# A fused transformer block, forward and backward: two weight transposes and two gates move, and the b2 gradient is summed by ScalarE

## The chip, the cores and the metric

The kernel runs on one core of one Trainium2 chip. TensorE (PE in the profile, with its weight loads as PEld), VectorE (DVE), ScalarE (ACT), GpSimd (POOL) and SyncE (SP) each run their own instructions in order and wait for each other through semaphores. SP, POOL and ACT also issue the DMAs. The metric is the device time of one execution in microseconds, taken as the median of several.

## The reference

The program computes the output of one pre-layernorm block and the gradients of its inputs and weights for a given output gradient (sequence S = 2048, width D = 512, F = 1792, 32 heads of 16; all bf16):

```python
q, k, v = qkv[0], qkv[1], qkv[2]                 # of layernorm(x) @ wqkv
idx = pos[:, None] - (arange(8) * 2)[None, :]    # each row sees itself and 7 earlier rows, 2 apart
logits = where(idx >= 0, einsum("bhsd,bhswd->bhsw", q, k[idx]) * scale, -1e9)
h  = x + einsum("bhsw,bhswd->bhsd", softmax(logits), v[idx]) @ wo
h2 = h + (gelu(layernorm(h) @ w1 + b1) @ w2 + b2)
out, vjp = jax.vjp(f, x, wqkv, wo, w1, b1, w2, b2)
return out, *vjp(grad_out)
```

The gradient of b2 is the sum of grad_out over all 2048 rows: 512 numbers.

## The kernel before, in words

The sequence is cut into four chunks of 512 rows (c = 0 to 3), each of four tiles of 128 rows. The forward pass, about the first 300 us, interleaves the attention of one chunk with the feed-forward part of the one before. For a chunk, `f_attn` forms products of q and k on DVE (L313), sums them on PE against a selection matrix (L320), and makes the softmax on DVE and ACT; the attention weights go to a DRAM buffer `at_r` (POOL queue, L442). `f_o` reads them back in another layout (`a4`, four SP DMAs, L300), multiplies with rows of v on DVE (`pbo`, L330), sums on PE (L336), copies on ACT (L451) and transposes. `f_h` adds the residual and makes the second layernorm. `f_ffn1` is the first FFN matmul with the activation spread over ACT (L508, L510, L518) and DVE (L515, L516, L520); the tensors u, s and g are stored to DRAM for the backward pass. `f_ffn2` is the second FFN matmul (L535).

Between the chunks of the forward pass, `turn_w` transposes the three blocks of wqkv and then wo on PE (L492), copies them on ACT (L493) and stores them for the last stage. The SBUF room of wqkv (tag `wq`) is later that of `w2T`, so w2T can only be written when the last read of wqkv is over. `w2T` and `w1T`, the transposed FFN weights for the backward pass, are each made by one DMA that transposes on its way (L602, L632). Both are issued on the SP queue.

The backward pass has three parts. From about 293 to 505 us, `b1_gg` and `b1_gx` go back through the FFN chunk by chunk in the order 3, 0, 1, 2: `make_goutT` transposes a chunk of the output gradient `gout` on PE into PSUM and copies it out on ACT (`to_T`, two copies of 1024 columns per chunk, L276); then come matmuls with w2T (L697), DVE work, transposes (L706) and matmuls with w1T (L719). `gw2_gen` fills in the gradient of w2 (L667), for which SP loads `gtm` by transposing DMAs (L664). At its start it also makes the gradient of b2: 16 matmuls with a column of ones as the weights (L659), a copy (L660) and a store (L661). Then the attention's backward pass follows: products on DVE (L330) with sums on PE, copied by ACT into `gt` (`b_sum`, L861 and L863), with the gradients of w1, wo and wqkv as fill on PE (L788, L918, L929). At the end `b_gx` (L892) makes the input gradient; for chunks 2 and 3 two of its three operands come through DRAM: a store to `gq_d` (POOL, L875) and a transposing DMA into `gTo` (SP, L876).

The order on each engine is fixed when the program is built: a scheduler moves instructions by priority, so an edit in one place can change the order around it. SP's DMAs also stand in one fixed order, and a DMA that waits holds back those behind it. `gate(ins, key)` adds a wait of `ins` for an earlier instruction recorded in `mark`; it is used to begin a transfer later than its data would allow.

Of the kernel before, what the change touches and what calls it, by code (L numbers as in the profile page):

```python
# [10 lines left out]
P = 128  # L11
BF16 = mybir.dt.bfloat16
F32 = mybir.dt.float32
ACT = mybir.ActivationFunctionType
ALU = mybir.AluOpType
AX = mybir.AxisListType
# [9 lines left out]
CH = 512  # L26
# [9 lines left out]
def kernel(  # L36
# [20 lines left out]
    nc = tc.nc  # L57
# [4 lines left out]
    S, D = xf.shape  # L62
    F = B_w1.shape[1]
    NT = S // P
    NC = S // CH
    TC = CH // P
    DC = D // P
# [7 lines left out]
    scale = DH ** -0.5  # L75

    def pool(name, bufs, side="left", space=None):
        kw = {} if space is None else {"space": space}
        return tc.alloc_tile_pool(name=name, bufs=bufs, side=side, reuse_waits="tile", **kw)
# [10 lines left out]
    const = ctx.enter_context(tc.tile_pool(name="const", bufs=1))  # L90
# [4 lines left out]
    def acc(name, tag="A"):  # L95
        return psum.tile([P, CH], F32, name=name, tag=tag, bufs=1 if tag in "TU" else 2)

    def ptile(name, tag="T"):
        return psum.tile([P, 8 * P], BF16, name=name, tag=tag, bufs=1 if tag in "TU" else 2)
# [4 lines left out]
    sync, pq = nc.sync, nc.gpsimd  # L104
    mark = {}
# [5 lines left out]
    def gate(ins, key):  # L111
        behind(ins, mark[key])


    ident = const.tile([P, P], BF16, name="ident")
# [7 lines left out]
    nc.vector.memset(one_t[:], 1.0)  # L123
    ones_row = const.tile([1, P], BF16, name="ones_row")
    nc.vector.memset(ones_row[:], 1.0)
    ones_col = const.tile([P, 1], BF16, name="ones_col")
    nc.vector.memset(ones_col[:], 1.0)
    rstd1 = const.tile([P, NT], F32, name="rstd1")
    rstd2 = const.tile([P, NT], F32, name="rstd2")
    b1c = const.tile([P, FT], F32, name="b1c")  # L130
# [26 lines left out]
    def pv(d_t):  # L157
        return d_t[:, :].rearrange("p (t d) -> p t d", t=TC)
# [26 lines left out]
    fw = pool("fw", 1, side="right")  # L185
# [79 lines left out]
            nc.vector.tensor_scalar(out=dst[:, j, :], in0=src[:, j, :], scalar1=mv[:, j, 0:1],  # L265
                                    scalar2=r[:, j:j + 1], op0=ALU.subtract, op1=ALU.mult)

    def to_T(src, dst, nm, tag, tag2=None):
        for d2 in range(DC // 2):
            pt = ptile(f"pt{nm}{d2}", tag2 if tag2 and d2 else tag)  # L270
            for i in range(2):
                for j in range(TC):
                    dc = 2 * d2 + i
                    nc.tensor.transpose(pt[:, (i * TC + j) * P:(i * TC + j + 1) * P],  # L274
                                        src[:, j, dc * P:(dc + 1) * P], ident[:])
            nc.scalar.copy(out=dst[:, 2 * d2:2 * d2 + 2, :], in_=pt[:].rearrange("p (i t) -> p i t", i=2))  # L276


    def four(eng, pool_, d_t, t0, nj, name, tag, bufs, step, key=None):
# [177 lines left out]
    def f_h(c):  # L457
        x, oT = load_x(c, "xr"), oTs.pop(c)
        h = fb.tile([P, TC, D], BF16, name=f"h{c}", tag="h", bufs=2)
        for j in range(TC):  # L460
            ps = acc(f"psh{c}_{j}")
            for g in range(G):
                nc.tensor.matmul(ps[:], lhsT=oT[:, g, j * P:(j + 1) * P], rhs=wo[:, g, :], start=(g == 0), stop=(g == G - 1))
            nc.vector.tensor_tensor(out=h[:, j, :], in0=ps[:], in1=x[:, j, :], op=ALU.add)
        ln2 = fr.tile([P, TC, D], BF16, name=f"ln2_{c}", tag="t1", bufs=1)
        layernorm(h, ln2, rstd2, c, "b")
        pq.dma_start(out=pv(ln2_d[c]), in_=ln2[:])
        ln2T = fl.tile([P, DC, CH], BF16, name=f"ln2T{c}", tag="ln2T", bufs=2)
        to_T(ln2, ln2T, f"b{c}", "U")
        hs[c], l2T[c] = h, ln2T  # L470
# [71 lines left out]
    def take(gen, n=1):  # L542
        for _ in range(n):
            next(gen, None)
# [46 lines left out]
    f_h(1)  # L591
    f_attn(2)
    turn_w = turn_w_gen()
    take(turn_w, 2)
    zero_pads(((q_r, S), (go_r, S), (at_r, S), (gl_r, S)), ("e", 1, 0))
    mix(f_ffn1(1), f_ffn2(0))
    f_o(2)
    f_h(2)
    take(turn_w, 2)
    f_attn(3)  # L600
    w2T = fw.tile([P, DC, F], BF16, name="w2T", tag="wq", bufs=1)
    gate(sync.dma_start_transpose(out=w2T[:], in_=B_w2[:, :]), ("e", 3, 1))  # L602
    mix(f_ffn1(2), f_ffn2(1))
    f_o(3)
    f_h(3)
# [1 line left out]
    br1 = pool("br1", 1, side="right")  # L607
    b1_order = (3, 0, 1, 2)
    gout, goutT = {}, {}
# [3 lines left out]
    place(br1, [P, TC, 2 * P], BF16, "th", 3)  # L613
    place(br1, [P, NT, P], BF16, "gtm", 2)
    place(br1, [P, D], BF16, "ow2", 3)
    gb2 = br1.tile([1, D], BF16, name="gb2")
    for c in b1_order:
        gout[c] = br1.tile([P, TC, D], BF16, name=f"gout{c}")
    br2 = pool("br2", 1, side="right")

    def load_gout(c):
# [4 lines left out]
    def make_goutT(i):  # L626
        if i < NC:
            c = b1_order[i]
            goutT[c] = get(br1, [P, DC, CH], BF16, f"goutT{c}", "goutT", 2)
            to_T(gout[c], goutT[c], f"e{c}", "T")  # L630

    w1T_load = sync.dma_start_transpose(out=w1T[:], in_=B_w1[:, :])  # L632
    gate(w1T_load, ("r", 3))
    mix(f_ffn1(3), f_ffn2(2))
    fl.release()

# [17 lines left out]
        nc.vector.tensor_tensor(out=out_ap, in0=u[:], in1=resid, op=ALU.add)  # L654

    def gw2_gen():
        ps = acc("psb2", "A")
        for t in range(NT):
            nc.tensor.matmul(ps[0:1, :], lhsT=ones_col[:], rhs=gout[t // TC][:, t % TC, :], start=(t == 0), stop=(t == NT - 1))  # L659
        nc.scalar.copy(out=gb2[:], in_=ps[0:1, :])  # L660
        nc.scalar.dma_start(out=out_7.rearrange("(a d) -> a d", a=1), in_=gb2[:])  # L661
        for ft in range(FT):
            gtm = get(br1, [P, NT, P], BF16, f"gtm{ft}", "gtm", 2)
            sync.dma_start_transpose(out=gtm[:], in_=g_d[ft * P:(ft + 1) * P, :])  # L664
            ps = acc(f"psw2{ft}", "U")
            for t in range(NT):
                nc.tensor.matmul(ps[:], lhsT=gtm[:, t, :], rhs=gout[t // TC][:, t % TC, :],  # L667
                                 start=(t == 0), stop=(t == NT - 1))
            ow = get(br1, [P, D], BF16, f"ow2{ft}", "ow2", 3)
            nc.scalar.copy(out=ow[:], in_=ps[:])  # L670
            pq.dma_start(out=out_6[ft * P:(ft + 1) * P, :], in_=ow[:])
            yield
# [100 lines left out]
    def load_tmx(f0, nf):  # L773
        tag = ("tm0", "tm2", "tm6", "tm2")[(f0 + 2) // 4]
        tmx = tmxs[f0] = (bg if f0 == 6 else bt).tile([P, NT, nf * P], BF16, name=f"h1tm{f0}", tag=tag, bufs=1)
        pq.dma_start(out=tmx[:], in_=tm(h1tm_d[:, f0 * P:(f0 + nf) * P]))
# [29 lines left out]
    for i in range(1, NC):  # L806
        load_ln2a(i)
        for n, _ in enumerate(b1_gg(i)):
            take(gw2, 1 if n in (2, 5) else 0)
            if n == 3 and i == 1:  # L810
                gate(sync.dma_start(out=woT[:], in_=wo_d[:, :].rearrange("p (j d) -> p j d", j=DC)), ("y", 1, 3))
        if i == NC - 1:
            br2.release()
            bt = pool("bt", 1)
            load_tmx(0, 2)
            load_tmx(2, 4)
            mix(b_go(0), none)
            b_ga(0)
        for n, _ in enumerate(b1_gx(i)):
            take(gw2, 1 if n == 1 else 0)  # L820
        if i > 1:
            mix(b_go(3 if i == 2 else 1), none)
# [24 lines left out]
    def b_sum(c, sel):  # L847
        sg = 0 if sel == 0 else 1
        d_a = at_r if sel == 2 else gl_r
        d_r, t_r = ((k_r, PAD - 2), (q_r, 0), (go_r, 0))[sel]  # L850
        nja = CJ + 2 * sg
        a4 = att4(bs_, d_a, CJ * c, nja, f"ba{sel}_{c}", "ba", 2, sg)
        gt = gvt[c] if sel == 2 else bp.tile([P, TC, D], BF16, name=f"gt{sel}_{c}")
        gts[sel, c] = gt
        for qd in range(Q4):
            r4 = row4(bs_, d_r, qd, t_r + CJ * c, CJ + 2, f"r4_{sel}{c}{qd}", "w4", W4B, sg)
            ps = acc(f"pss{sel}{c}_{qd}", "A")
            wsum(bs_, ps, a4, r4, sg, f"{sel}{c}_{qd}", 200)
            o_ap, i_ap = gt[:, :, qd * P:(qd + 1) * P], ps[:].rearrange("p (j m) -> p j m", j=TC)
            if sel == 2:  # L860
                mark["s", c, 2] = mark["s", c, 2, qd] = nc.scalar.copy(out=o_ap, in_=i_ap)  # L861
            else:
                mark["s", c, sel] = nc.scalar.activation(out=o_ap, in_=i_ap, func=ACT.Copy, scale=scale)  # L863
            yield

    gTs, rooms = {}, []

    def b_gT(c):

        if not rooms:  # L870
            rooms.append(bg.tile([P, NC, DC, CH], BF16, name="gTo", tag="tm6", bufs=1))
        for i, sel in enumerate((2, 0)):
            gTs[sel, c] = rooms[0][:, 2 * (c % 2) + i]
            d_t = gq_d[sel][c]
            gate(pq.dma_start(out=d_t[:, :].rearrange("(j p) d -> p j d", p=P), in_=gts[sel, c][:]), ("s", 2, 1))  # L875
            gate(sync.dma_start_transpose(out=gTs[sel, c], in_=d_t[:, :]), ("s", 3, 1))  # L876

    def b_gx(c):
        gT = {}
# [57 lines left out]
    for c in range(NC):  # L937
# [4 lines left out]
        if c == 2:  # L942
            load_otm()
            load_ln1a(bl, (0, 1, 2), ("g", 3, 0))
            for sel in range(3):
                gate(pq.dma_start(out=wqkvT[:, sel * DC:(sel + 1) * DC, :],
                                  in_=wqkv_d[sel][:, :].rearrange("p (j d) -> p j d", j=DC)), ("g", 3, 0))
# [12 lines left out]
    wg, wq, wk = gwqkv_gen(2), gwqkv_gen(0), gwqkv_gen(1)  # L960
# [54 lines left out]
```

## Time and profile before

| | us |
|---|---|
| median of 5 runs | 714.5 (714.32 to 716.25) |
| the profiled execution | 714.81 |
| its span | 712.3 |
| PE / DVE / ACT / POOL busy | 629.3 / 556.2 / 395.4 / 210.6 |
| w2T transposing DMA: issue, landing | 211.2, 16.6 after |
| w1T transposing DMA: issue, landing | 261.8, 17.3 after |
| first matmul with w2T / with w1T | 293.7 / 321.8 |
| the b2 gradient's matmuls | 338.2 to 345.9 |
| gTo transposing DMAs: issue | 670.0 to 680.4 |

Times in the profile count from the start of the span. A group's line reads: source line, engine, operation, output<-input, shapes, count, then busy time, mean duration of one in ns, and the idle time of the engine just before with what ended it. A timeline's line reads: start, duration, engine, line, operation, and in brackets the idle time before it and what ended that. "SPq" rows are DMA issues on the SP queue. Line numbers in all profile rows are those of the kernel that was profiled.

### The profile page before, as it was taken

What the parts mean: (1) busy time and instruction counts of PE and PEld (TensorE: products, weight loads), DVE (VectorE), ACT (ScalarE), POOL (GpSimd) and SP (SyncE); (2) the same over time, 40 slices, a digit from 0 to 9 for tenths busy, and PEclk for the clock granted to TensorE, in tenths of its full rate; (3) what the DMA queues carried; (4) which work ended last, traced back from release to release, by engine and by line L of the source; (5) the groups of instructions that cost most, each with busy time, mean ns of one, the idle gap of its engine ahead of it and who ended that gap; (6) DMA issues with size and microseconds to landing.
All of it is one profiled execution on the core that took longest, in us unless ns stands there. A gap on an engine that the chain in (4) does not pass through costs nothing. (4 is left out here: it accounts for less than half of the span.)

```text
span 712.3 us, 10332 instructions
## 1 busy us (share of the span) xinstructions
PE 629.3 (88%) x3682; PEld 265.1 (37%) x3682; DVE 556.2 (78%) x919; ACT 395.4 (56%) x548; POOL 210.6 (30%) x318
## 2 busy tenths in 40 slices
PE   1898667779789489999999999998999999999985
PEld 0433222234334134444444444443533333334432
DVE  6467958778972858975988888476899999999754
ACT  5554334878957639945867687552131135357543
POOL 4324333434433443443452433313200410001000
PEclk9999897979989789999999999999999999999999
DMA  8497698664879659567674985859899999986642
GB/s 237 137 266 236 179 367 290 225 260 155 247 295 242 205 162 218 180 197 277 185 222 107 181 209 142 263 108 239 301 354 365 322 344 290 351 284 209 165 102 67
DMA packets 103221, 163.57 MB, mean 230 GB/s; under 512 B 60961, under 2 KB 69250, under 8 KB 103170
## 3 DMA queue, kind: packets, MB, share of 16 engines
q1 hardware_dynamic: 73824, 78.40, 39.7%
q0 software_dynamic: 24720, 80.07, 34.5%
q10 hardware_dynamic: 4626, 4.46, 1.9%
q8 instruction: 28, 0.46, 0.3%
q14 instruction: 23, 0.19, 0.1%
HBM read 90.97 MB, written 56.71 MB: 207 GB/s over the span
## 5 line engine op out<-in xcount | busy, mean ns | idle before, releaser
L330 DVE TENSOR_TENSOR pb<-ba,r 128x2048 bf16<-128x2048 bf16 x96 | 111.5, 1220 | 0.8 <-PE pss L336 0.7
L506 PE MATMUL psf<-ln2T,w 128*128 128x512 bf16 x224 | 59.0, 400 | 12.3 <-ACT u L508 12.2
L535 PE MATMUL ps<-w,g 128*128 128x512 bf16 x224 | 55.7, 379 | 0.0
L788 PE MATMUL psw<-h1tm,ln2a 128*128 128x512 bf16 (+1 forms) x256 | 54.3, 354 | 0.0
L667 PE MATMUL psw<-gout,gtm 128*128 128x512 bf16 x208 | 51.3, 379 | 2.4 <-DMA gtm<-g_d 1.6
L719 PE MATMUL psx<-w1T,gh 128*128 128x512 bf16 x216 | 50.4, 379 | 0.0
L330 DVE TENSOR_TENSOR pbo<-a,v 128x2048 bf16<-128x2048 bf16 x32 | 38.2, 1217 | 15.1 <-DMA a<-at_r 10.2
L372 ACT CAST qkv<-psq 128x512 bf16<-128x512 f32 x48 | 27.6, 586 | 33.3 <-PE psq L370 26.5
L697 PE MATMUL psg<-goutT,w2T 128*128 128x512 bf16 x168 | 42.3, 379 | 0.0
L508 ACT ACTIVATE u<-psf,b1c 128x512 bf16<-128x512 f32 x56 | 36.1, 682 | 8.6 <-PE psf L506 5.3
L506 PEld LDWEIGHTS <-w 128*128 128x128 bf16 x224 | 21.0, 101 | 42.1 <-issue 24.7
L710 POOL DMA_DIRECT2D h1tm_d<-th x27 | 20.9, 772 | 52.5 <-ACT th L708 37.6
L518 ACT ACTIVATE s<-z 128x1024 bf16<-128x1024 bf16 x28 | 29.6, 1060 | 10.5 <-DVE z L516 7.3
L863 ACT ACTIVATE gt<-pss 128x512 bf16<-128x512 f32 x32 | 19.1, 597 | 28.9 <-PE pss L336 28.9
L313 DVE TENSOR_TENSOR pag<-go,bv 128x2048 bf16<-128x2048 bf16 x24 | 28.6, 1219 | 8.2 <-PE ga L320 4.5
L708 ACT COPY th<-pth 128x1024 bf16<-128x1024 bf16 x27 | 27.0, 1000 | 11.1 <-PE pth L706 11.1
L788 PEld LDWEIGHTS <-ln2a 128*128 128x128 bf16 x256 | 22.6, 98 | 27.6 <-issue 10.2
L689 ACT ACTIVATE by<-bu 128x1024 bf16<-128x1024 bf16 x21 | 22.2, 1057 | 19.1 <-DVE gb1p L699 16.4
L929 PE MATMUL psq<-gt,ln1a 128*128 128x512 bf16 x128 | 32.0, 380 | 0.0
L892 PE MATMUL psy<-wqkvT,gT 128*128 128x512 bf16 x128 | 31.8, 379 | 0.3 <-DVE lua L653 0.2
L526 POOL DMA_DIRECT2D g_d<-g x28 | 20.5, 733 | 37.1 <-DVE g L520 35.0
L336 PE MATMUL pss<-pb,sel 128*32 128x512 bf16 x384 | 29.5, 384 | 0.7 <-DVE pb L330 0.5
(221 smaller groups left out, 1365.3 us busy)
## 6 DMA issues: line engine op xcount, KB each, us to landing
v<-v_r SPq DMA_DIRECT2D x16, 576.0 KB, 7.1
r<-go_r SPq DMA_DIRECT2D x16, 576.0 KB, 7.8
r<-k_r SPq DMA_DIRECT2D x16, 576.0 KB, 6.4
r<-q_r SPq DMA_DIRECT2D x16, 576.0 KB, 5.1
g_d<-g POOLq DMA_DIRECT2D x28, 256.0 KB, 4.1
h1tm_d<-th POOLq DMA_DIRECT2D x27, 256.0 KB, 4.6
h1tm<-h1tm_d POOLq DMA_DIRECT2D x3, 2048.0 KB, 12.4
x_d<-u POOLq DMA_DIRECT2D x21, 256.0 KB, 5.3
```

The lines of the kernel that those rows point to most:

```text
L330: last = nc.vector.tensor_tensor(out=pr[:], in0=_ap(a_ap, [a_ap.ap[0], [2 * H, CJ], [0, Q4], [1, H]], off=wh * H + (4 * H * wh if sg else 0)),
L336: mm = nc.tensor.matmul(ps[PR * n:PR * n + PR, :], lhsT=sel4[:], rhs=prs[wh][:, TC * n:TC * n + TC, :, :].rearrange("p j d h -> p (j d h)" ...
L506: nc.tensor.matmul(ps[:], lhsT=w1[0][:, dc, ft * P:(ft + 1) * P], rhs=ln2T[:, dc, :], start=(dc == 0), stop=(dc == DC - 1))
L508: nc.scalar.activation(out=u[:, i, :], in_=ps[:], func=ACT.Identity, bias=b1c[:, ft:ft + 1], scale=1.0)
L518: nc.scalar.activation(out=s[:], in_=z[:], func=ACT.Sigmoid, scale=2.0 * GC)
L535: nc.tensor.matmul(ps[:], lhsT=gs[ft // 2][:, ft % 2, j * P:(j + 1) * P], rhs=w2[0][:, ft, :], start=(ft == 0), stop=False)
L667: nc.tensor.matmul(ps[:], lhsT=gtm[:, t, :], rhs=gout[t // TC][:, t % TC, :], start=(t == 0), stop=(t == NT - 1))
L697: nc.tensor.matmul(ps[:], lhsT=w2T[:, dc, ft * P:(ft + 1) * P], rhs=gT[:, dc, :], start=(dc == 0), stop=(dc == DC - 1))
L719: nc.tensor.matmul(ps[:], lhsT=t1s[ft // 2][:, ft % 2, j * P:(j + 1) * P], rhs=w1T[:, ft, :], start=(ft == 0), stop=(ft == FT - 1))
L788: nc.tensor.matmul(ps[:, 0:nf * P], lhsT=ln2a[:, t // TC, t % TC, dc * P:(dc + 1) * P], rhs=tmx[:, t, 0:nf * P], start=(t == 0), stop=(t = ...
L892: nc.tensor.matmul(ps[:], lhsT=gT[sel][:, g, j * P:(j + 1) * P], rhs=wqkvT[:, sel * G + g, :], start=(n == 0), stop=(n == NJ - 1))
L929: nc.tensor.matmul(ps[:], lhsT=ln1a[t // TC][:, t % TC, dc * P:(dc + 1) * P], rhs=gts[sel, t // TC][:, t % TC, :], start=(t == 0), stop=(t ...
```

## The change

The change has four parts.

- Three blocks instead of two are transposed by `turn_w` before `f_ffn1(1)`, and only the fourth, wo, after `f_h(2)`. The w2T DMA is issued before `f_attn(3)`, gated on the last residual addition of chunk 1, instead of after `f_attn(3)` and gated on its last exponential.
- The gate of the w1T DMA is the last copy of `f_o(3)` instead of the second layernorm's rstd of chunk 3.
- The b2 gradient no longer uses PE's matmuls with ones. `to_T` for the output gradients copies 512 columns at a time (four instructions per chunk instead of two), each with an accumulator output that sums over the 512 rows of the chunk. After the last chunk DVE adds the four partial sums and casts, PE transposes the [128, 4] result, ACT copies it and POOL stores it.
- The gTo DMAs of chunk 2 are gated on the first of the last four gt copies, those of chunk 3 on the third, instead of all on the fourth.

```diff
-    ones_col = const.tile([P, 1], BF16, name="ones_col")
-    nc.vector.memset(ones_col[:], 1.0)
...
-    def to_T(src, dst, nm, tag, tag2=None):
+    def to_T(src, dst, nm, tag, tag2=None, sums=None):
...
-            nc.scalar.copy(out=dst[:, 2 * d2:2 * d2 + 2, :], in_=pt[:].rearrange("p (i t) -> p i t", i=2))
+            if sums is None:
+                nc.scalar.copy(out=dst[:, 2 * d2:2 * d2 + 2, :], in_=pt[:].rearrange("p (i t) -> p i t", i=2))
+            else:
+                for i in range(2):
+                    nc.scalar.activation(out=dst[:, 2 * d2 + i, :], in_=pt[:, i * CH:(i + 1) * CH], func=ACT.Copy,
+                                         accum_out=sums[:, 2 * d2 + i, :])
...
-            nc.vector.tensor_tensor(out=h[:, j, :], in0=ps[:], in1=x[:, j, :], op=ALU.add)
+            mark["h", c] = nc.vector.tensor_tensor(out=h[:, j, :], in0=ps[:], in1=x[:, j, :], op=ALU.add)
...
     turn_w = turn_w_gen()
-    take(turn_w, 2)
+    take(turn_w, 3)
     zero_pads(((q_r, S), (go_r, S), (at_r, S), (gl_r, S)), ("e", 1, 0))
     mix(f_ffn1(1), f_ffn2(0))
     f_o(2)
     f_h(2)
-    take(turn_w, 2)
+    take(turn_w, 1)
+    w2T = fw.tile([P, DC, F], BF16, name="w2T", tag="wq", bufs=1)
+    gate(sync.dma_start_transpose(out=w2T[:], in_=B_w2[:, :]), ("h", 1))
     f_attn(3)
-    w2T = fw.tile([P, DC, F], BF16, name="w2T", tag="wq", bufs=1)
-    gate(sync.dma_start_transpose(out=w2T[:], in_=B_w2[:, :]), ("e", 3, 1))
...
-    gb2 = br1.tile([1, D], BF16, name="gb2")
     for c in b1_order:
         gout[c] = br1.tile([P, TC, D], BF16, name=f"gout{c}")
+    gb2p = br1.tile([P, DC, NC], F32, name="gb2p")
+    gb2s = br1.tile([P, DC], F32, name="gb2s")
+    gb2b = br1.tile([P, DC], BF16, name="gb2b")
+    gb2r = br1.tile([DC, P], BF16, name="gb2r")
...
-            to_T(gout[c], goutT[c], f"e{c}", "T")
+            to_T(gout[c], goutT[c], f"e{c}", "T", sums=gb2p[:, :, c:c + 1])

     w1T_load = sync.dma_start_transpose(out=w1T[:], in_=B_w1[:, :])
-    gate(w1T_load, ("r", 3))
+    gate(w1T_load, ("o", 3, 3))
...
     def gw2_gen():
-        ps = acc("psb2", "A")
-        for t in range(NT):
-            nc.tensor.matmul(ps[0:1, :], lhsT=ones_col[:], rhs=gout[t // TC][:, t % TC, :], start=(t == 0), stop=(t == NT - 1))
-        nc.scalar.copy(out=gb2[:], in_=ps[0:1, :])
-        nc.scalar.dma_start(out=out_7.rearrange("(a d) -> a d", a=1), in_=gb2[:])
...
         if i == NC - 1:
             br2.release()
             bt = pool("bt", 1)
+            nc.vector.tensor_reduce(out=gb2s[:], in_=gb2p[:], axis=AX.X, op=ALU.add)
+            nc.vector.tensor_copy(out=gb2b[:], in_=gb2s[:])
+            pth = ptile("ptg2", "T")
+            nc.tensor.transpose(pth[0:DC, 0:P], gb2b[:, :], ident[:])
+            nc.scalar.copy(out=gb2r[:], in_=pth[0:DC, 0:P])
+            pq.dma_start(out=out_7.rearrange("(dc p) -> dc p", p=P), in_=gb2r[:])
...
-                mark["s", c, sel] = nc.scalar.activation(out=o_ap, in_=i_ap, func=ACT.Copy, scale=scale)
+                mark["s", c, sel] = mark["s", c, sel, qd] = nc.scalar.activation(out=o_ap, in_=i_ap, func=ACT.Copy, scale=scale)
...
-            gate(sync.dma_start_transpose(out=gTs[sel, c], in_=d_t[:, :]), ("s", 3, 1))
+            gate(sync.dma_start_transpose(out=gTs[sel, c], in_=d_t[:, :]), ("s", 3, 1, 2 * (c - 2)))
```

## The prediction

> **What bounds the kernel now.** I read the page first (busy shares and the 40 slices), then the mean clock and DMA share by stretch, then the timelines of each engine around each transfer that the diff touches. The chain that ended last covers only the final 26 us (it begins at 681.26), so each stage was read from its own timeline. From the page:
>
> ```profile
> PE 629.3 (88%) x3682; PEld 265.1 (37%) x3682; DVE 556.2 (78%) x919; ACT 395.4 (56%) x548; POOL 210.6 (30%) x318
> PE   1898667779789489999999999998999999999985
> DVE  6467958778972858975988888476899999999754
> PEclk9999897979989789999999999999999999999999
> DMA  8497698664879659567674985859899999986642
> ```
>
> No engine bounds all of it. Up to about 260 us (slice 15) PE has holes and a lowered clock: the interleave of attention and FFN is held by waits. From 260 to 505 PE is full (9 in nearly every slice); from 512 to 672 DVE is. The largest hole is after 228 us, seen by stretch (columns: stretch, length, then PE, PEld, DVE, ACT, POOL busy, granted clock, DMA share, GB/s):
>
> ```profile
> 165.00:175.00 10.00, 9.98 (x58) 3.99 (x59) 7.79 (x11) 8.54 (x11) 4.56 (x7) 1.00 0.47 143
> 211.00:220.00 9.00, 8.98 (x52) 3.98 (x51) 5.48 (x11) 5.63 (x8) 3.67 (x7) 1.00 1.07 236
> 220.00:228.00 8.00, 8.00 (x38) 3.46 (x37) 2.48 (x5) 6.84 (x9) 3.64 (x5) 1.00 1.14 216
> 228.00:237.00 9.00, 2.88 (x13) 1.00 (x12) 5.45 (x8) 3.48 (x5) 1.61 (x3) 0.87 0.46 168
> ```
>
> DMA is full from 211 to 228, then all engines starve. The timelines of the SP queue, DVE, ACT and PE say why:
>
> ```profile
> 211.19 9.72 SPq L602 DMA_TRANSPOSE w2T<-in_B_w_dram  x1
> 226.96 2.39 SPq L300 DMA_DIRECT2D a<-at_r  x4
> 231.55 1.23 DVE L330 TENSOR_TENSOR pbo<-a,v 128x2048 bf16<-128x2048 bf16 x1 [6.41 <-DMA a<-at_r]
> 235.48 1.06 ACT L518 ACTIVATE s<-z 128x1024 bf16<-128x1024 bf16 x1 [5.49 <-DVE z L516]
> 237.16 3.57 PE L506 MATMUL psf<-ln2T,w 128*128 128x512 bf16 x8 [6.29 <-ACT u L508]
> ```
>
> The w2T transpose lands 16.6 us after issue. Chunk 3's attention weights are written to at_r by POOL at 215.1 to 217.3, beside it, and read back (`a`) behind it. DVE reaches its product with `a` at 225.1 and waits 6.41; DVE runs in order, so the FFN's `z` stands behind it, then ACT, then PE. The same at_r writes in chunk 2, without a transpose, and then in chunk 3, with it:
>
> ```profile
> DMA to landing us min/median/max: 2.0/2.1/2.4
> DMA to landing us min/median/max: 8.6/8.9/10.2
> ```
>
> The last stage has the like: the gTo transposes are issued once the last gt copy is done, and PE waits.
>
> ```profile
> 670.04 4.45 SPq L876 DMA_TRANSPOSE gTo<-gq_d  x2
> 679.49 1.04 PE L892 MATMUL psy<-wqkvT,gTo 128*128 128x512 bf16 x4 [2.64 <-DMA gTo<-gq_d]
> ```
>
> **The change part by part** (positions in the built program, durations from the profiled execution).
>
> 1. *w2T leaves 211 us.* DVE, ACT and PE all stand still there, so the 6.41 is on the path. Without it: at_r issued by 217.3, landing 2.1, `a` issued over 2.4 and landing 2.4, so ready at about 224, before DVE is free at 225.1. Ends: -8.1 (6.4, and PE's eight matmuls at 237.16 taking 1.9 as elsewhere instead of 3.57 at the clock lowered by the hole) and -1.5 (if at_r lands as the stores at 190 to 200 do, 7.0 to 8.5, though no transpose runs there). The chunk 2 row is the same operation, so I take -6.4. What is late next: the xr loads, of which PE's psh has need only after the sums.
>
> 2. *w2T goes in front of chunk 2's `a` load on SP.* It now waits for the last of wqkv's PE transposes, 16 of which (a third block) move ahead of ffn1(1) and stand inside the first two rows of ffn2(0). The second block ran at 157.4 and 159.1; the third follows after a row's rest, so w2T issues at about 163.2. Behind it on SP stand chunk 2's `a` loads, then v, out and xr. With the old distance from w2T's issue to the usable `a` (231.55 - 211.19 = 20.4), `a` is there at 183.6. DVE used it at 179.61; in the new order pa, g and a z go ahead of it, the z needing ACT's square (done at 181.4), so DVE arrives at about 181.5. Stall: 2.1. Ends: 0 (at_r lands in 2.1 after all, DMA share being 0.47 there) and +6.4 (as before at chunk 3). ACT's two copies (1.02 and 1.07 at 186.6 and 197.8, where ACT is 95 to 100% busy) move to 161 to 165, where it waited 2.0 for PE: 0 to -2.1, I take -1.1. Their 16 matmuls cost PE 16 x 0.06, hidden in the same waits. Together +1.0.
>
> The rows first: at_r's landing grew from 2.1 to 8.9 beside the transpose. The Trainium skill ("DMA: Bandwidth & Descriptors", "Issuing engines are not separate DMA queues") says that DMAs of all issuing engines run on the same 16 DMA engines and interleave, which speaks against the change: a transpose moved is a collision moved. By that rule alone chunk 2 would pay what chunk 3 saves, and the sum would be 5.4 us higher; the DMA share of 0.47 against 1.07 speaks for less.
>
> 3. *w1T's gate* moves from rstd (issue at 261.80) to chunk 3's last L451 copy (251.28, done 251.9), ten us earlier. It lands in 17.3. PE is full from 257.8 and first needs it at 321.8; the stretch 250 to 262 has a DMA share of 0.39. The gout and ln stores around 264 are freed of it, but nobody waits for them. 0; ends -1 and +1 (PE's waits of 0.7 at 262, and the stores of chunk 2's last s and g at 253).
>
> 4. *The b2 gradient leaves PE.* Sixteen matmuls against ones:
>
> ```profile
> L659 PE MATMUL psb<-gout,ones_col 128*1 128x512 bf16 x16 | 4.1, 378 | 0.0
> 343.61 2.32 PE L659 MATMUL psb<-gout,ones_col 128*1 128x512 bf16 x10
> ```
>
> Pipelined, (2.32 - 0.38) / 9 = 0.216 each, so 16 x 0.216 = 3.45, in a stage where PE idles 6.9 us of 215. Ends -3.45 and -1.7 (half soaked up by waits for DVE). I take -3.45. The copy and store of gb2 were beside other work.
>
> 5. *ScalarE's sums.* Per chunk two copies of 1.01 become four of 0.597 plus four accumulator reads of 0.196 (ACT's L646 rows; the pair takes 0.69 back to back): 2.76 against 1.9, +0.9. For the first two chunks ACT is 93% busy (290 to 300) and PE waits for these copies already:
>
> ```profile
> 296.91 0.61 PE L274 MATMUL pte<-ident,gout 128*128 128x128 bf16 x8 [0.97 <-ACT goutT_first L276]
> ```
>
> There +1.0 (ends 0 and +1.8); the later two have ACT at 5 to 8 tenths: 0. At the end a small reduce, cast, PE transpose, copy and POOL store: nearest rows are gb1's (0.22 on PE, 0.20 on DVE), +0.3, ends 0 and +1.
>
> 6. *gTo's gates.* The pairs now wait for the first and the third of the last four gt copies (657.94 and 665.74) instead of the last (669.41). The gq_d stores are issued 656.5 to 659.5 and land in 3.7 to 6.0, so the four issue from about 662, 2.2 each, and land in 4.3 to 7.4: by 676. PE's uses are at 675.8 and 676.9, so -2.6; ends 0 and -2.64, since PE has no other gap there. The last r loads stand ahead of them on SP, the gx store behind: nobody waits for it.
>
> 7. *Order.* On SP the transpose of gtm12 now precedes bv and go of chunk 1 (issued at 484.8 and 485.5): up to 2 later, where DVE waits 1.99 for go; in return PE's wait of 1.64 for gtm goes, and with it part of DVE's 3.72 behind it. 0; ends -1.6 and +2.
>
> Sum: -6.4 + 1.0 - 3.45 + 1.0 + 0.3 - 2.6 = -10.2. The profiled execution took 714.81 (span 712.3 and 2.5 around it), 0.3 above the median of 714.5: 714.81 - 10.2 - 0.3 = 704.3, rounded to 704.5.
>
> **Rivals.**
> - *The stall only moves.* Chunk 2 waits 6.4 as chunk 3 did. For: the at_r writes stand 5 us behind w2T's issue, as they stood 4 behind before. Against: DMA 0.47, and DVE has more to do first. 704.5 + 5.4 = 709.9.
> - *Only the stall counts.* PE's matmuls and the gTo wait are replaced by others (DVE's sums in 293 to 505, gx in the end): 704.5 + 3.45 + 2.6 = 710.5. For: PE often waits 0.2 for gb1p. Against: PE at 98%.
> - *Slower.* w2T, first in line on SP, comes so late that `a` of chunk 2 holds DVE long: each us of issue after 161.1 (181.5 - 20.4) is a us lost. It turns the sign when that stall exceeds 12.3 (2.1 and the 10.2 saved), that is at an issue after 173.4 instead of 163.2; at 176 (stall 14.9, that is 12.8 more than taken) the time is 717.3. For: its PE transposes wait for ACT copies, and ACT is 85% busy from 165. Against: they stand before ffn1(1) in PE's order.
>
> **How the numbers follow.** Forecast 0.56 (own range 700 to 709), stall moved 0.19, only the stall 0.11, slower 0.09, and 0.05 for more than all terms at their best. The best ends (-8.1, -2.1, -1, -3.45, 0, 0, -2.64, -1.6) sum to -18.9, which needs all at once; I set the low end at 699, and the high end at 713, beyond both middling rivals. A measurement tells about 0.2%, 1.4 us, from no change: faster 0.85 (forecast, the middling rivals with little left out, the better tail), same 0.05 (their upper edges), slower 0.10 (the third rival and a little of those edges).
>
> **What would show it.** w2T issued near 163 and `a` of chunk 3 used without a wait of DVE; no PE hole of 6 us near 231 and a clock at 1.0 there; a DVE wait of some 2 us at chunk 2's first pbo; L659 gone and b1 shorter by 3; no gTo wait on PE. Wrong if DVE waits over 6 us at chunk 2, if b1 (293 to 505) keeps its length, or if PE waits at the last psy on something else.

## The result and the profile after

The changed kernel takes 718.68 us (median of 27 runs, 712.92 to 724.95), the kernel before, run beside it, 713.66 us (48 runs, 709.1 to 718.78). The ratio is 1.0063, 95% interval 1.0044 to 1.0082: slower by 4.5 us, where 704.5 was predicted. The ratios are taken over the executions within 1.5% of each kernel's fastest; the medians of all differ by 5.0. The profiled execution took 715.37 us (span 713.6), 3.3 below its median, against 714.81 before. So these two traces show only part of the difference, and a place counts below where several kernels show it.

From the page of the changed kernel:

```profile
PE 624.9 (88%) x3667; PEld 263.7 (37%) x3667; DVE 554.2 (78%) x920; ACT 396.9 (56%) x572; POOL 209.5 (29%) x319
PE   1898666869759889899989999999999999999995
PEclk9998897979989999999999999999999999999999
```

PE has 15 instructions fewer and is 4.4 us less busy. The end is not earlier: work was taken away, and the time stayed as waiting. Where the stall went is seen by stretch (columns as in the prediction):

```profile
165.00:175.00 10.00, 10.00 (x65) 4.26 (x64) 8.55 (x14) 7.92 (x11) 4.30 (x8) 1.00 1.08 192
175.00:182.00 7.00, 7.00 (x37) 2.50 (x39) 6.25 (x9) 5.93 (x7) 1.94 (x4) 1.00 1.06 220
182.00:189.00 7.00, 5.36 (x33) 1.92 (x25) 0.23 (x2) 4.46 (x5) 2.82 (x4) 1.00 0.86 297
228.00:237.00 9.00, 9.00 (x42) 3.88 (x41) 6.24 (x10) 8.91 (x13) 3.59 (x5) 1.00 0.49 169
```

The hole at 228 is gone: PE is full there and its clock is 1.00 instead of 0.87. There is a new one at 182 to 189, in which DVE works 0.23 us; in the kernel before DVE was full there:

```profile
182.00:189.00 7.00, 5.89 (x52) 2.82 (x50) 7.00 (x10) 6.49 (x9) 3.78 (x6) 1.00 0.90 284
```

The DMA share ahead of it (165 to 175), 0.47 before, is now 1.08. The timelines of the SP queue, DVE, ACT and PE of the changed kernel:

```profile
164.90 12.45 SPq L604 DMA_TRANSPOSE w2T<-in_B_w_dram  x1
182.22 2.39 SPq L303 DMA_DIRECT2D a<-at_r  x4
188.86 1.23 DVE L333 TENSOR_TENSOR pbo<-a,v 128x2048 bf16<-128x2048 bf16 x1 [6.78 <-DMA a<-at_r]
190.72 1.06 ACT L521 ACTIVATE s<-z 128x1024 bf16<-128x1024 bf16 x1 [3.21 <-DVE z L519]
191.88 1.04 PE L339 MATMUL pso<-pbo,sel 128*32 128x512 bf16 x8 [4.52 <-DVE pbo L333]
```

The picture that chunk 3 had (wait for `a`, then z, then ACT, then PE) now stands in chunk 2, as long as before: 6.78 against 6.41. The POOL stores to at_r for chunk 2, which took 2.1 to land, now take

```profile
DMA to landing us min/median/max: 10.2/10.7/11.3
```

That is the rule which the prediction weighed and discounted. The Trainium skill ("DMA: Bandwidth & Descriptors", "Issuing engines are not separate DMA queues") says that DMAs started by different engines interleave on the same 16 DMA engines; here stores of POOL's queue take five times as long to land beside a transpose of SP's.

The second place is the backward FFN. The group of gw2's matmuls waits 6.1 us, against 2.4 before:

```profile
L668 PE MATMUL psw<-gout,gtm 128*128 128x512 bf16 x208 | 51.2, 379 | 6.1 <-DMA gtm<-g_d 4.3 <-ACT ow L671 1.7
```

In the timelines of SP, PE and DVE:

```profile
345.31 0.35 SPq L812 DMA_DIRECT2D woT<-wo_d  x1
346.08 16.75 SPq L665 DMA_TRANSPOSE gtm<-g_d  x2
361.07 0.60 PE L668 MATMUL psw<-gout,gtm 128*128 128x512 bf16 x2 [3.00 <-DMA gtm<-g_d]
482.56 7.85 SPq L665 DMA_TRANSPOSE gtm<-g_d  x2
491.22 0.51 SPq L285 DMA_DIRECT2D go<-go_r  x1
497.77 4.63 DVE L316 TENSOR_TENSOR pag<-go,bv 128x2048 bf16<-128x2048 bf16 x4 [4.88 <-DMA go<-go_r]
```

PE takes up the third gtm in the middle of b1. Before, its load was issued at 348.26 and first used at 367.35, with no wait. With the 16 matmuls gone and PE's fill reordered, PE is ready for it at 358.07 (361.07 less the wait), nine us sooner, and the load goes out only two us sooner, right behind woT. At 482 two gtm transposes go ahead of chunk 1's go, which is issued at 491.22 instead of 485.46; DVE waits 4.88 for it instead of 1.99.

The last stage did what was forecast. The gTo DMAs are issued from 665.85 on (670.04 before), and PE takes them up without a wait:

```profile
665.85 10.65 SPq L883 DMA_TRANSPOSE gTo<-gq_d  x4
679.76 1.89 PE L899 MATMUL psy<-wqkvT,gTo 128*128 128x512 bf16 x8
```

The same instructions in several traces (us; experiments below; "o" is DVE's addition behind each second FFN matmul, "gx" DVE's first operation on each gradient of b1, `jlf<-psx,ln2a`; rs#1 to rs#2 is from the second to the third `rs` on DVE in the attention's backward pass, the stretch that waits for chunk 1's go):

| | before | after | w2T alone | b2 alone | b2, go first | sums added | b2 left out | gTo alone |
|---|---|---|---|---|---|---|---|---|
| first o of ffn2(0) to first o of ffn2(2) | 99.12 | 96.99 | 95.77 | 98.50 | 96.83 | 96.09 | 98.96 | 96.38 |
| first o of ffn2(2) | 263.11 | 262.48 | 259.97 | 261.19 | 261.99 | 261.12 | 265.26 | 262.08 |
| from the latter to the first gx | 63.26 | 65.94 | 64.42 | 65.94 | 65.91 | 65.98 | 63.14 | 63.79 |
| first gx to last gx | 142.47 | 142.29 | 142.57 | 146.15 | 140.29 | 144.47 | 137.32 | 142.58 |
| rs#1 to rs#2 | 15.72 | 17.93 | 15.78 | 20.29 | 15.83 | 15.07 | 17.48 | 17.27 |

### The profile page after: what moved, and what is told of

It is laid out like the page before. It is cut to its first block, busy times and chain, and to the rows that moved or that the text cites. A ratio compares the mean times of both kernels' runs of the same rounds, so it can differ in the third digit from the quotient of the medians.

```text
span 713.6 us, 10326 instructions
## 1 busy us (share of the span) xinstructions
PE 624.9 (88%) x3667; PEld 263.7 (37%) x3667; DVE 554.2 (78%) x920; ACT 396.9 (56%) x572; POOL 209.5 (29%) x319
## 5 line engine op out<-in xcount | busy, mean ns | idle before, releaser
L333 DVE TENSOR_TENSOR pbo<-a,v 128x2048 bf16<-128x2048 bf16 x32 | 38.2, 1218 | 14.6 <-DMA a<-at_r 11.3
L316 DVE TENSOR_TENSOR pag<-go,bv 128x2048 bf16<-128x2048 bf16 x24 | 28.6, 1220 | 10.2 <-DMA go<-go_r 6.6
L339 PE MATMUL pso<-pbo,sel 128*32 128x512 bf16 x128 | 16.1, 432 | 18.8 <-DVE pbo L333 16.8
L700 DVE CUSTOM_DVE_ANT_0 gh<-psg,by 128x512 bf16<-128x512 f32 x42 | 27.8, 686 | 4.9 <-PE psg L698 4.6
```

What stands on the lines that cost most here:

```text
L316: nc.vector.tensor_tensor(out=pr[:], in0=_ap(q_ap, [q_ap.ap[0], [P, 2], [0, W], [1, P]]), in1=_ap(k_ap, [k_ap.ap[0], [P, 2], [-DIL * P, W] ...
L333: last = nc.vector.tensor_tensor(out=pr[:], in0=_ap(a_ap, [a_ap.ap[0], [2 * H, CJ], [0, Q4], [1, H]], off=wh * H + (4 * H * wh if sg else 0)),
```

## The experiments

My theory after the result: the w2T part gains nothing because the collision moved with the transpose, and the b2 part costs more than it saves because DMAs on SP change places around it. Rival A: the ScalarE sums are the loss. Rival B: w2T was only put in the wrong place, and another place gives the 6.4 us. A ratio is that to the kernel before on the same chip, with its 95% interval.

### Each part by itself

**b2_alone** holds only the third part of the change.

```diff
-            to_T(gout[c], goutT[c], f"e{c}", "T")
+            to_T(gout[c], goutT[c], f"e{c}", "T", sums=gb2p[:, :, c:c + 1])
...
-            nc.tensor.matmul(ps[0:1, :], lhsT=ones_col[:], rhs=gout[t // TC][:, t % TC, :], start=(t == 0), stop=(t == NT - 1))
```

> The kernel before with only the b2 part of the change: ScalarE's sums instead of the 16 matmuls with ones. Theory (the freed 3.45 us of PE are given back to waits for transposing loads: PE waits 3.0 for gtm near 361, and go of chunk 1, now behind two gtm transposes on SP, holds DVE 4.9 instead of 2.0 near 493): +2 to +4 us against the kernel before, with both waits in its trace. Rival A (ScalarE's sums are the price, the removed matmuls a true gain, the loss of the changed kernel lies in the forward pass): -2.5 to 0 us, no such waits.

719.73 us against 714.6: 1.0070 (1.0045 to 1.0095), 5.0 us slower. This part alone is the loss. By stretch, the kernel before and then this one:

```profile
355.00:365.00 10.00, 9.86 (x60) 4.70 (x58) 7.89 (x19) 6.90 (x8) 4.97 (x7) 1.00 0.92 277
```

```profile
335.00:345.00 10.00, 9.95 (x62) 4.84 (x61) 8.57 (x22) 8.32 (x14) 1.23 (x2) 1.00 0.01 2
345.00:355.00 10.00, 9.58 (x55) 4.47 (x55) 8.40 (x19) 7.49 (x9) 5.44 (x8) 1.00 1.04 187
355.00:365.00 10.00, 4.94 (x22) 2.33 (x21) 3.55 (x9) 1.61 (x4) 3.42 (x5) 0.72 1.07 195
```

and its SP and PE timelines:

```profile
344.01 0.34 SPq L812 DMA_DIRECT2D woT<-wo_d  x1
344.79 20.09 SPq L665 DMA_TRANSPOSE gtm<-g_d  x2
361.76 1.03 PE L668 MATMUL psw<-gout,gtm 128*128 128x512 bf16 x2 [4.99 <-DMA gtm<-g_d]
```

For ten us hardly anything is moved (share 0.01: POOL's queue stands 14.6 us behind one store). Then POOL's stores and loads, woT and the transpose start within a few us, the DMAs are full, and the third gtm arrives 17 us after issue. The loads of bu and bs that feed b1 land in 10.0 and 14.2 us instead of 4.3 and 5.4 (medians of those issued before 349), so DVE starves too. PE is half idle, and the granted clock of the stretch falls to 0.72. The kernel before has the same pause and the same burst (POOL stands 14.24 there), but its transpose goes out 5.0 us behind woT, not 0.8.

**w2t_alone** holds only the first part: w2T behind a third transposed block and gated on chunk 1's residual.

```diff
-    gate(sync.dma_start_transpose(out=w2T[:], in_=B_w2[:, :]), ("e", 3, 1))
+    gate(sync.dma_start_transpose(out=w2T[:], in_=B_w2[:, :]), ("h", 1))
```

> The kernel before with only the w2T part: three wqkv blocks turned ahead of chunk 1's first FFN matmul and the w2T transpose issued near 165 instead of 211. Theory (the wait for the attention weights moves whole from chunk 3 to chunk 2: 6.8 against 6.4 us): -1.5 to +1 us against the kernel before. Rival A (the loss of the changed kernel is here, the earlier hole costs more than the later one): +3 to +5 us. The prediction had -5.4.

716.08 against 715.65: 1.0009 (0.9972 to 1.0046). DVE waits for `a` in chunk 2:

```profile
185.72 1.23 DVE L330 TENSOR_TENSOR pbo<-a,v 128x2048 bf16<-128x2048 bf16 x1 [4.60 <-DMA a<-at_r]
```

In this execution the stall is 1.8 shorter than chunk 3's was. The trace is 3.1 us ahead of the one before at 263 (table), but that shows no gain: ten traces of kernels with w2T at its old place lie between 259.12 and 265.26 there. From ffn2(0) to ffn2(2) those ten take 96.1 to 99.1, this one 95.8 and the changed kernel 97.0, so little or nothing of the 6.4 is won in the forward pass.

**w1t_alone** and **gto_alone** hold the second and the fourth part.

```diff
-    gate(w1T_load, ("r", 3))
+    gate(w1T_load, ("o", 3, 3))
```

> The kernel before with only the gate of the w1T transpose moved ten us earlier. Theory: -1 to +1 us, since PE needs it 50 us later. Rival: +2 us or more, from the stores and loads of chunk 3's residual and layernorm near 252 to 270 that then share the DMA engines with it.

716.12 against 715.65: 1.0008 (0.9976 to 1.0039): nothing.

```diff
-            gate(sync.dma_start_transpose(out=gTs[sel, c], in_=d_t[:, :]), ("s", 3, 1))
+            gate(sync.dma_start_transpose(out=gTs[sel, c], in_=d_t[:, :]), ("s", 3, 1, 2 * (c - 2)))
```

> The kernel before with only the gates of the four gTo transposes moved to the first and third of the last four copies. Theory: -2 to -2.7 us, the PE wait of 2.64 near 677 gone. Rival: 0, another wait of PE in its place.

712.85 against 715.65: 0.9969 (0.9940 to 0.9998), 2.2 us faster; the one version run that leaves nothing out and has both its median and its interval below the kernel before, and so below the changed one. PE's wait of 2.64 for gTo is gone from its trace. By the ratios the four parts come to +0.6 + 5.0 - 2.2 + 0.6 = +4.0 us, and the whole change to +4.5: they add up within their intervals.

### What the b2 part loses

**b2_sums_added** keeps the 16 matmuls and adds the sums, which nobody uses; **b2_left_out** has neither and stores zeros for the gradient of b2.

```diff
-            to_T(gout[c], goutT[c], f"e{c}", "T")
+            to_T(gout[c], goutT[c], f"e{c}", "T", sums=gb2p[:, :, c:c + 1])
```

> The kernel before with ScalarE's sums added to its copies of the transposed output gradients, while the 16 matmuls with ones stay and still make the b2 gradient; the sums are not used. It prices the sums alone. Theory: +0.5 to +1.5 us (the first two chunks' copies, where PE waits for them already). Rival A: +3 us or more.

```diff
+    nc.vector.memset(gb2[:], 0.0)
...
-        for t in range(NT):
-            nc.tensor.matmul(ps[0:1, :], lhsT=ones_col[:], rhs=gout[t // TC][:, t % TC, :], start=(t == 0), stop=(t == NT - 1))
```

> The kernel before with the b2 gradient left out altogether (zeros are stored in its place): no matmuls with ones, no sums, and the old order of go and gtm. It prices the removal of 3.45 us of PE work alone. Theory: -1 to 0 us, because PE then waits for the third gtm transpose, which lands late beside the stores and loads of POOL, for most of what it saved. Rival A: -3 to -3.5 us, as the prediction took it.

Sums added: 715.68 against 714.6, 1.0026 (0.9998 to 1.0054), +1.9. Left out: 706.49 (six runs), 0.9894 (0.9857 to 0.9930), -7.6, more than twice the 3.45 of the matmuls. So rival A explains some two of the five us (its interval reaches from -0.1 to 3.9): -7.6 + 1.9 would be a gain of 5.7, and b2_alone loses 5.0. By this subtraction the rest lies in the order that comes with both; the runs below look for the place. With b2 left out the third gtm is issued at 342.40, ahead of woT, lands in some 7 us, and PE doesn't wait; the gTo wait falls to 0.45 as well. Of the 7.6, 3.45 are the matmuls and 2.2 that wait; the rest I can't place. The profiled execution is the slowest of the six (711.17), so its trace doesn't hold all of the 7.6.

**b2_go_first** undoes one order in b2_alone: the transpose of gtm12 waits for chunk 1's go.

```diff
+            if ft == 12:
+                gate(tr, ("go4", 1))
```

> As the run with the b2 part alone, but the thirteenth gtm transpose waits for the issue of chunk 1's go load, so SP has bv and go ahead of it as in the kernel before; nothing else differs in the orders. Theory: the go wait falls from 4.9 to about 2, so 2.5 to 4 us less than the b2 part alone, within 1 us of the kernel before or up to 1.5 better. Rival A: the order is worth under 1 us.

717.31 against 714.6: 1.0052 (1.0017 to 1.0086). DVE's wait for go is 1.92 (5.80 in b2_alone) and its stretch 15.83 instead of 20.29 (15.1 to 17.5 in the kernels of the table whose wait for go is some 2 us); the time is 1.3 us less than b2_alone's by the ratios and 2.4 by the medians, but the intervals overlap. My expectation that nothing else would differ was wrong: the gate moved PE's order too, and DVE waits 2.67 for `pss` ahead of 520.

**b2_wot_only** and **b2_wot_later** issue woT one chunk later, without and with that gate. **b2_out_wot_first** is b2_left_out with woT put ahead of the third gtm.

```diff
-            if n == 3 and i == 1:
-                gate(sync.dma_start(out=woT[:], ...), ("y", 1, 3))
+            if n == 3 and i == 2:
+                gate(sync.dma_start(out=woT[:], ...), ("y", 2, 3))
```

> The b2 part alone with woT's load a chunk later, and go still behind the thirteenth gtm. Theory: the gtm wait near 360 goes, 3 to 5 us less than the b2 part alone, so 0 to +2 us against the kernel before. Rival A: as the b2 part alone, +4 to +6.

> As the run with the b2 part and go first, and woT's load (512 KB, first used near 414) is gated a chunk later: near 383 instead of 344, so that the third gtm transpose no longer stands right behind it. Theory (the third gtm lands in 13 to 20 us because it shares the DMA engines with woT and the loads of bu and bs; where b2 was left out it stood ahead of woT and landed in 7): no PE wait for gtm over 0.5 near 360, 3 to 6 us less than the run with go first, that is 0 to -3 us against the kernel before. Rival C (ScalarE's sums or the changed order of the fill work cost it): still +2 to +4 us.

```diff
+            if ft == 2:
+                gate(tr, ("y", 1, 3))     # the key that woT's load is gated on
```

> The b2 gradient left out (zeros stored in its place) as in the earlier run, with one change: the third gtm transpose is gated so that woT's load stands ahead of it on SP, as in the changed kernel; the orders on PE, DVE, ACT and POOL are the same. Theory (the late third gtm takes back the freed PE time): PE waits 2 to 5 us for gtm near 350 to 360, and 3 to 5 us of the 7.6 gained are lost. Rival A (the order is worth nothing, the sums and what they delay cost it all): within 1 us of the run that left b2 out.

b2_wot_only: 714.09 against 713.83, 0.9994 (0.9963 to 1.0025), 5 us better than b2_alone, and the two intervals don't overlap. The third gtm lands in at most 8.6 us and PE has no wait for it:

```profile
344.58 10.97 SPq L665 DMA_TRANSPOSE gtm<-g_d  x2
356.52 0.59 PE L668 MATMUL psw<-gout,gtm 128*128 128x512 bf16 x2
```

The two kernels differ in woT's place alone. In their traces DVE, ACT and POOL's DMAs keep the same order, on SP only woT moves, and PE differs only by 67 records that b2_alone's trace lacks, spread from its start to its end. So the five us that b2_alone loses hang on woT's place. With the load in time b1 (first to last gx) takes 139.55, 2.9 less than before, so there the removed matmuls are a gain; the sums (2.8 up to the first gx) and a wait of 6.15 for go stand against it.

b2_wot_later: 717.32 against 714.76, 1.0019 (0.9985 to 1.0054). It differs from b2_go_first in woT's place alone, but here the intervals overlap. Its trace is 4.2 ahead at the last gx, 4.0 of it already at 263, and loses it between 505 and 540, with the `pss` wait of 2.67 again.

b2_out_wot_first: 706.73 against 713.83, 0.9900 (0.9865 to 0.9935), as fast as b2_left_out and with the same order on PE, DVE and ACT. woT goes out at 344.67 and the third gtm at 345.13; the last of its packets in the trace is 7.7 after issue, and PE takes it up at 359.48 with no wait. That fells the theory that woT's place is enough. DMA was not idle before it there (share 0.27 at 335 to 345), and POOL stands 8.0 us instead of 14.6.

Read together: POOL's burst and the transpose without woT do no harm (b2_wot_only), nor do woT and the transpose without the long pause and the burst (b2_out_wot_first). With all at once the third gtm takes 13.4 (b2_go_first), 15.0 (the changed kernel) and 17.0 us (b2_alone). With five us between woT and the transpose its last packet comes after 7.5 us before, but after 11.3 with the sums added, and both were in time for PE. woT's part is shown by one edit. The part of the pause and the burst is argued: no run takes them out of b2_alone, and b2_out_wot_first has another PE order.

### Is there a better place for w2T?

**w2t_behind_a** gates w2T on the landing of chunk 3's `a`.

```diff
+    gate(sync.dma_start_transpose(out=w2T[:], in_=B_w2[:, :]), "a")     # after f_o(3)
```

> The kernel before with the w2T transpose moved the other way: it waits for the landing of chunk 3's attention weights (about 225 to 231) and stands right behind them on SP; all else as before. Theory (the wait exists because at_r's store and load share the DMA engines with the transpose, wherever that stands ahead of them): no DVE wait over 2 us for the attention weights in chunk 2 or 3, -4 to -7 us. Rival B (the hole is only displaced again, to the residual loads or the stores after 231): -2 to +1 us.

715.46 against 715.65: 0.9992 (0.9963 to 1.0022). The wait for `a` is gone, and the hole is back some seven us on, at the stores whose buffers ACT needs:

```profile
223.35 12.06 SPq L604 DMA_TRANSPOSE w2T<-in_B_w_dram  x1
235.65 1.06 ACT L518 ACTIVATE s<-z 128x1024 bf16<-128x1024 bf16 x1 [4.03 <-DMA s_d<-s]
```

**w2t_at_250** gates it on the third of chunk 3's last L451 copies, and **w2t_gto** adds the gTo gates to that. **w2t_then_w1t** is w2t_at_250 with w1T waiting for w2T's landing, **w2t_w1t_gto** the same with the gTo gates.

```diff
+    gate(sync.dma_start_transpose(out=w2T[:], in_=B_w2[:, :]), ("o", 3, 2))     # after f_h(3)
...
-    gate(w1T_load, ("r", 3))
+    behind(w1T_load, w2T_load)     # the two ..._w1t kernels
```

> The kernel before with the w2T transpose gated on the third of chunk 3's last copies, behind the residual loads on SP: near 242 to 248, where the DMA engines are 0.36 to 0.40 busy until w1T at 260. Theory (a transposing DMA of this size costs 4 to 7 us wherever DVE, ACT or PE soon need another transfer, and nothing where they don't): no DVE or ACT wait over 2.5 us from 205 to 263, -3 to -6 us. Rival B (it collides again, with w1T and the output gradient's loads behind it): PE waits near 290 for the output gradient or w2T, -1 to +2 us.

> The w2T transpose near 245 and the earlier gTo gates together on the kernel before; the b2 gradient by matmuls with ones. Theory: the sum of the two, -5 to -8 us. Rival: under 3 us gained, what the first saves being waited for again at a transfer of the later stages.

> As the run with w2T near 245, but w1T waits for w2T's landing, so the two transposing loads never overlap (the b2 gradient by matmuls with ones, gTo gates as before). Theory (the two in flight together held each other up: 19.0 us to issue w2T, 31.5 to issue w1T, gtm 20.9 us late): w1T lands in 17 to 20 us, PE waits under 3 us near 283 to 290, -3 to -6 us against the kernel before in every execution. Rival (there is no room for both ahead of the backward pass): PE waits for gtm or w1T near 290 to 320 and nothing is gained.

> The same with the earlier gTo gates. Theory: 2 to 2.7 us below the run without them, -5 to -8.5 us in all. Rival: as that run.

All four spread widely from one execution to the next: 706.4 to 730.6 (median 726.0), 706.7 to 727.4 (721.3), 718.9 to 740.5 (727.3) and 704.2 to 733.1 (715.9; twelve executions), against 714 to 715 before (medians, since a ratio would speak for a part of them only). The forward pass does gain: from the first o of ffn2(0) to that of ffn2(2) the traces of these four take 91.1 to 91.8 us, against 96.1 to 99.1 with w2T at its old place. Six of the 30 executions (704.2 to 709.1) lie below every execution of the kernel before beside them. In the profiled ones the queue is blocked afterwards, as the SP and PE timelines of w2t_at_250 show (its slowest execution, 730.62):

```profile
242.55 19.03 SPq L605 DMA_TRANSPOSE w2T<-in_B_w_dram  x1
261.69 31.47 SPq L632 DMA_TRANSPOSE w1T<-in_B_w_dram  x1
304.09 2.31 PE L667 MATMUL psw<-gout,gtm_first 128*128 128x512 bf16 x5 [20.87 <-DMA gtm_first<-g_d]
```

gtm_first stands behind w1T on SP, and w1T lands 37.2 us after issue instead of 17.3. Waiting for w2T first doesn't help by itself: in the profiled execution of w2t_then_w1t, the slowest of its six, w1T takes 33.5 and PE waits 27.49; in that of w2t_w1t_gto, up to there the same plan, w1T takes 17.7 and PE waits 7.38.

**gtm_before_w1t** puts the first two gtm ahead of w1T and chunk 2's output stores behind it, with the gTo gates; **gtm_before_w1t_b2** adds the b2 part with woT later, and **all_mended** is w2t_gto with all of b2_wot_later.

```diff
+        if n == 2:
+            mark["w1T"] = sync.dma_start_transpose(out=w1T[:], in_=B_w1[:, :])
+            gate(mark["w1T"], ("gg", 3, 2))
```

> w2T near 245, then on SP the first two gtm transposes, then w1T (gated on the third product g of chunk 3, near 275) and only then the stores of chunk 2's output; the earlier gTo gates; the b2 gradient by matmuls with ones. Theory (what failed near 245 was the gtm load standing behind w1T): PE waits under 3 us for gtm_first, w1T lands before its first use near 315, -6 to -9 us against the kernel before with little spread. Rival (no room for three transposing loads between 245 and 315): PE waits over 5 us for gtm or w1T, no gain, a wide spread.

> The same with ScalarE's sums for b2 and woT a chunk later. Theory: within 1.5 us of the run without the sums (the b2 part with woT later measured 0.9994 of the kernel before). Rival: 3 us or more slower than it, by the sums' delay of the first copies near 290 or by go behind gtm near 490.

> All of it: w2T near 245, the earlier gTo gates, ScalarE's sums for b2 with go first and woT later. Theory: -6 to -10 us. Rival: no better than the same without the sums, because ScalarE's sums cost what the 16 matmuls did.

715.81 against 714.78, 0.9993 (0.9954 to 1.0032); 717.05 against 714.78, 1.0035 (1.0004 to 1.0065); and 705.8 to 731.2 (median 722.8, six executions). In gtm_before_w1t the gtm land in time, and PE waits 6.22 and 5.25 for the loads of gout instead. So rival B holds for the forward pass and for single executions, but no place that was tried gives the gain in the median: in each trace an engine waited for a load or store beside or behind w2T, or the w1T that follows it.

## Why the prediction was wrong, step by step

The prediction had -5.4 for the w2T part and -2.15 for the b2 part; by themselves they measured +0.6 and +5.0. These two make 13 of the 14.7 us between -10.2 and +4.5. The rival "slower" had the sign, but for another reason: it needed a stall of over 12.3 at chunk 2, and that stall is 6.78.

- *Step 1, w2T leaves 211 us: right.* `a` of chunk 3 is used with no wait, and the clock is 1.00.
- *Step 2, w2T ahead of chunk 2's `a`: failed.* DVE arrives at 182.08, as worked out (181.5), but the stall is 6.78 and not 2.1: w2T issues 1.7 later than taken, and `a` is usable 24.0 after that instead of 20.4, its at_r stores landing in 10.7. The upper end of the step (6.4) was the value, and the rival "the stall only moves" held for this part. (By the step's own terms that rival costs 6.4 - 2.1 = 4.3 and not 5.4, since the -1.1 for ACT's copies stays.) The error was to price the collision by the DMA share of 0.47 in a stretch that did not yet hold the transpose.
- *Step 3, w1T's gate at 0: right* (1.0008).
- *Step 4, -3.45 for the matmuls: right in size as work removed, wrong as time saved.* b1 (first to last gx) keeps its length, 142.29 against 142.47. The step costed the matmuls as if PE's order stayed; they were also what PE did while the third gtm was loaded. With them gone and the fill reordered, PE came for it nine us sooner, and waited 3.00 (4.99 in b2_alone). Where that load is in time (b2_wot_only), b1 is 2.9 shorter, near the 3.45.
- *Step 5, sums at +1.0 (ends 0 and +1.8): too small.* +1.9 by the time of b2_sums_added. In the traces the stretch from 263 to the first gx is 2.7 longer in each of the four kernels of the table with sums, and 1.2 longer at most in the others. The pieces cost what was taken (0.58 to 0.60 and 0.19 to 0.21 for the accumulator), but ACT's other work stands between the halves, and it waits 0.69 and 0.88 for PE: the copies of the first two chunks run from 291.37 to 302.82 instead of 292.01 to 300.43. The +0.3 for the end was not measured by itself.
- *Step 6, -2.6 for gTo: right* (-2.2 alone, wait gone). In b2_alone 0.38 of this wait is left without the gates, but 2.11 in b2_go_first, so whether the two parts overlap here is open.
- *Step 7, order at 0 (ends -1.6 and +2): wrong end.* DVE's wait for go grew by 2.9, in b2_alone by 3.8, where the stretch is 4.6 longer; the gate that undoes it brings both back. That the third gtm now goes out directly behind woT was not in the step at all, and it is the costliest omission: with woT a chunk later the 5.0 of the b2 part are gone (b2_wot_only).

Open: the rest of what leaving b2 out gains, whether POOL's pause and burst are needed for the late gtm, why the transfers slow each other so much, and what spreads the kernels with w2T at 242.

## What to carry to other kernels

A large transfer that is moved takes its collision along: price it by what is issued beside and behind it in the new place, with the stall it makes now, and not by how empty that place looks without it. Work that leaves a full engine also uncovers what was loading behind it: follow that engine's next few operands back to their loads, and look for each in the new order of the queue. Test the parts of a change one by one; here one part was worth keeping and was hidden under another that lost twice as much.

## What was not expected of the hardware

- The w2T transpose (512 x 1792 bf16, 1.8 MB) lands 14.9 to 19.4 us after issue where it stands between 160 and 215, some 95 to 123 GB/s by these numbers. Of two transposes close together (w2t_at_250) the second took up to 37.2, in a stretch (262 to 293) where the DMA share was 1.22 but 137 GB/s were moved; the kernel before moved 266 at a share of 1.01 (345 to 355). A full share says little of the rate. The Trainium skill ("DMA: Bandwidth & Descriptors", "Latency and other measured facts") gives 261 GB/s for a DMA transpose with a non-contiguous middle dimension, measured on one kernel; by that w2T would take an estimated 7 us, which no run here shows.
- One hole of 5 us in PE cost more than itself: in b2_alone the granted clock of its stretch fell to 0.72, and seven matmuls after it took 607 to 634 ns instead of 379.
- Two kernels with the same plan up to that point had a PE wait of 7.38 and of 27.49 at the same matmul. With transposes this close together, one trace does not stand for the median.
